# Threshold attention and a low-rank mixer on one core: every transpose of weights and u moved from the transfer engines to TensorE, and score steps paired across borders

## The chip, the core and the metric

The kernel runs on one core of one Trainium2 chip. The core has five engines that work through their own queues in order: TensorE (PE in the profile, with its weight loads as PEld), VectorE (DVE), ScalarE (ACT), GpSimd (POOL) and SyncE (SP), which issues transfers. Sixteen DMA engines move the data. The metric is the device time of one execution in microseconds (us).

## What is computed

Eight batches, eight heads, 576 rows, 64 columns per head. Attention keeps only the scores within tau of the row's largest, and its output goes through a mixer with a low-rank step over the rows and a two-layer network over the columns:

```python
def _attn_ref(q, k, v, tau):
    scores = scale * np.matmul(q, k.transpose(0, 1, 3, 2))
    thresh = np.max(scores, axis=-1, keepdims=True) - tau
    scores = np.where(scores >= thresh, scores, -1000000000.0)
    scores = scores - np.max(scores, axis=-1, keepdims=True)
    attn = np.exp(scores)
    attn = attn / (np.sum(attn, axis=-1, keepdims=True) + 1e-09)
    return np.matmul(attn, v)

def _moe_ref(x, U, V, w_ch1, w_ch2):
    h = x.transpose(0, 2, 1) @ U @ V              # rank 32, over the 576 rows
    u = x + h.transpose(0, 2, 1)
    return u + np.maximum(u @ w_ch1, 0.0) @ w_ch2  # 512 -> 2048 -> 512
```

q, k and v are float32; the result has shape 8 x 576 x 512 in float32.

## The kernel before

Heads are taken two at a time: four pairs of heads in each of 8 batches, 32 pairs `p`. A pair's 576 rows are four tiles of 128 and one of 64; two neighbouring pairs put their last 64 rows together, so a couple of pairs has nine score steps, and the kernel has 16 x 9 = 144. A step makes two tiles (one for each head, `x`) of 128x576.

The life of a step, with the lines of the profile:

- `scores` (L641): float32 matmuls of q and k into PSUM. A group has one step or two. PSUM has eight banks; a group of two steps takes the six of `trio`, a single group four. In the first couple all steps are single; in the other 15 couples the first is single and eight make four groups of two: 9 + 15 x 5 = 84 groups.
- `weigh` (L670, DVE): scales the scores out of PSUM, takes their extreme `m` along the row.
- `threshold` (L686, ACT): `m` plus tau. `exponential` (L693, ACT).
- `select` (L700, DVE): exponential where the score passes the threshold, else zero, into `w_ring` as bf16, with the row's sum into `den`.
- `twin` (L718, POOL): copies the last 64 columns once more, so that a tile has five blocks of 128.
- The turn, since the weighted sum needs keys on the partitions: `turn_w` (L724) is a transposing transfer on SP's queue; `turn_pe` (L731) is five matmuls against the identity into one bank, with a copy out of PSUM on ACT (`copy_w`, L741). In the kernel before, 25 of the 288 tiles go by PE: tile `x == 1` of steps 1 to 3 in the first `EARLY = 8` pairs, and one more. The other 263 go by 143 transfers, most of which take both tiles of a step.

`value_tasks` follows for each pair: the weighted sum `product` (L798 to 808) with v split in a high and a low bf16 part (`high` on ACT L600, `low` on POOL L607); the reciprocal of the sums (`inverse`, L774 and 776, DVE); for pairs 0 to 3 (`SOFT`) the product with it (L831), for the others a joining add (L859) and a product on POOL (L866); the low-rank step (L879, L894, L901); then u in bf16 (L908), which is turned for the mixer: in the first 8 pairs by PE and ACT (`turn_u` L916, `copy_u` L932), in the others by a transposing transfer (`send_u`, L922).

`mixer_tasks` of a batch has 16 tasks of four matmuls up (L998), the rests (L1014), with a relu on ACT (L988); then for each of nine row tiles of two batches four tasks of four matmuls down (L1031), a final sum on DVE (`finish`, L1043) and the store (L1054 to 1060, SP). These matmuls lie between the attention's on PE.

All of this is written down as tasks with an engine and what they depend on. Their order is not found at run time: `ORDER` is a list of task numbers, worked out beforehand, and `BANK` gives each PE task its PSUM bank. A negative number in `ORDER` is a filler matmul (L473) that computes nothing needed. Each engine's queue is in that order. q and k are loaded from POOL's queue for most pairs (L510), from SP's for pairs 1 and 2 (`LOADERS`); the mixer's weights come over POOL's queue, each held back by a `gate` on a score step.

Of the kernel before, what the change touches and what calls it, by code (L numbers as in the profile page):

```python
# [68 lines left out]
P = 128  # L69
FP32 = mybir.dt.float32  # L70
# [15 lines left out]
EARLY = 8  # L86
PHASES = (1, 2, 3, 4, 5, 6, 8, 28)
LONE = 2
LOADERS = (None, "SSSS", "SSSS")
ACTED = 0  # L90


W1_AT = (1, 4, 6, 9, 11, 14, 16, 19)
W2_AT = (20, 21, 23, 24, 25, 26, 28, 29)
# [14 lines left out]
PE, VEC, SCA, POOL, SP = range(5)  # L109
# [3 lines left out]
class Task:  # L113
# [17 lines left out]
    23, 21, 22, 25, 20, 26, 24, 19, 44, 28, 46, 40, 27, 29, 42, -1, -1, -1, -1, -1, -1, -1, -1, -1, 32, 41, 30, 33,  # L131
    43, 34, 31, 39, 35, 45, -2, -2, -2, 59, 201, 36, 200, 60, 37, 38, 204, 61, 63, -7, -7, -7, -7, -7, 69, 205, 62,
    65, 64, 206, 54, 70, 50, 198, 55, 52, 71, 203, 73, 218, 82, 66, 72, 202, 77, 222, 74, 199, 1, 83, 47, 67, 3, 84,
    49, 86, -3, -3, -3, -3, -3, -3, 95, 0, 78, 68, 85, 51, 87, 53, 90, 96, 75, 97, 219, 76, -8, -8, -8, -8, -8, -8,
    108, 91, 221, 98, 99, 2, 48, 211, 103, 109, 207, 209, 110, 112, 119, 100, 225, 212, 111, 104, 79, 114, 213, 120,
    92, 224, -3, 80, 121, 123, 220, -7, 129, 115, 125, 223, 113, 122, 4, 93, 131, 432, 56, 130, 101, 210, 88, 439,
    142, 89, 124, 137, 105, 81, 126, 57, 106, 102, 94, 143, 169, 132, 127, 144, 437, 146, 128, 155, 168, 214, 150,
    138, 107, 233, 170, 139, 231, 116, 157, 145, 438, 133, 117, 229, 156, 232, 457, 238, 134, 163, 455, 208, 151,
    158, 234, 171, 434, 230, 240, 159, 135, 58, 136, 239, 140, 244, 147, 152, 241, -6, 248, 141, 118, 172, 456, 242,
    245, 5, 243, 433, 153, 249, 453, 154, 250, 160, -8, -8, -8, -8, 173, 251, 164, 215, 161, 174, 256, 452, 261, -1,  # L140
    -1, -1, 184, 162, 148, 252, 262, 435, 264, 183, 149, 165, -4, 273, 257, 459, 175, 185, 246, 258, 253, 247, 216,
    274, 176, 254, 458, 275, 228, 177, 263, 268, 217, 286, -8, -8, 178, 255, 166, 259, 281, 179, 443, 454, 277, 269,
    188, 226, 436, 276, 287, 444, 227, 6, 180, 189, 265, 167, -3, -3, -3, -3, -3, -3, 181, 278, 288, 266, 289, 296,
    282, 270, 260, 267, 182, 290, 283, 291, 297, 441, 279, 271, 186, 292, 280, 300, 298, 272, 293, 345, 235, 440,
    344, 187, 299, 306, 294, 236, 302, 447, 445, 237, 307, 284, 448, 309, 346, 308, 301, 626, 446, 462, -2, -2, -2,
    318, 285, 303, 295, 190, 310, 304, 460, 313, 319, 191, 320, 9, 192, 322, -8, -8, 193, 331, 311, 347, 326, 624,
    312, 194, 321, 620, 334, 314, 349, 305, 195, 467, 348, 315, 625, 350, 468, 332, -4, 316, 351, 465, 333, 339,
    352, 335, 463, 353, 466, 196, 323, 336, 354, 317, 472, 355, 324, 464, 619, 325, 327, 356, 337, 622, 197, 474,
    357, 328, 338, 442, 623, 473, 364, 358, 461, 621, 329, 340, 475, 476, 482, 639, 359, 478, 341, 477, 640, 330,
    365, 8, 483, 342, 484, 360, 10, 343, 495, 7, 486, 362, 496, 449, 642, 479, 485, 507, 469, 363, 487, 490, 470,  # L150
    361, 498, 509, 480, 634, 366, 488, 481, 630, 471, 508, 632, 635, 631, 521, 367, 644, 633, 489, 520, 368, 497,
    511, -7, -7, 369, 491, 530, 522, 510, 370, 515, 492, 645, 499, 371, 887, 502, 531, 882, 372, 374, 532, 373, 12,
    493, 375, 494, 641, 380, 503, 533, 523, 376, 540, 504, 381, 11, 505, 525, 516, 378, 500, 377, 512, 886, 501,
    382, 506, 526, 450, 379, 384, 383, 541, 534, 13, 386, 524, 536, 513, 552, 535, 527, 514, 385, 537, 542, 883,
    387, 543, 528, 517, 538, 553, 646, 518, 547, 650, 554, 451, 519, 388, 529, 566, 555, 14, 390, 628, 565, 389,
    888, 651, 659, 544, 391, 556, 545, 884, 392, 546, 660, 560, 661, 394, 567, 568, 629, 548, 393, 669, 647, 561,
    395, 549, 539, 572, 557, 643, 665, 670, 562, 550, 558, 663, 648, 16, 396, 671, 551, 627, 885, 573, 398, 397,
    569, 672, 400, 662, 399, 682, 570, 673, 574, 402, 571, 881, 683, 401, 563, 674, 403, 652, 559, 654, 564, 578,
    577, 901, 598, 653, 666, 15, 655, 649, 575, 677, 694, 664, 579, 678, 685, 667, 580, 689, 679, 695, 581, 892,
    576, 696, 902, 684, 894, 698, 18, 707, 896, 582, 893, 690, 675, 897, 702, 586, 708, 676, 583, 599, 895, 584,  # L160
    587, 636, 585, 588, 717, 668, 686, 903, 600, 601, 589, 710, 691, 637, 712, 718, 17, 607, 590, 719, 603, 687,
    638, 697, 727, 608, 709, 680, 703, 656, 591, 904, 889, 692, 404, 699, 604, 907, 592, 890, 681, 609, 704, 406,
    602, 605, 688, 693, 728, 606, 405, 593, 765, 713, 906, 407, 723, 711, 908, 739, 766, 610, 594, 700, 611, 657,
    767, 701, 714, 595, 905, 740, 612, 658, 715, 912, 752, 613, 720, 596, 729, 614, 721, 741, 1048, 705, 911, 408,
    734, 1054, 722, 716, 597, 1049, 409, 724, 706, 1051, 753, 410, 742, 747, 725, 615, 1055, 726, 411, 730, 735,
    913, 914, 412, 743, 736, 769, 1053, 731, 915, 413, 616, 773, 744, 732, 770, 916, 737, 774, 748, 917, 617, 1072,
    755, 733, 921, 775, 754, 749, 764, 738, 771, 794, 776, 909, 618, 923, 768, 750, 795, 414, 922, 745, 759, 772,
    746, 796, 1068, 924, 415, 760, 751, 1071, 925, 891, 756, 931, 1050, 927, 926, 1052, 777, 785, 757, 932, 1075,
    786, 758, 933, 1070, 941, 778, 761, 934, 787, 416, 779, 942, 935, 780, 788, 898, 417, 781, 944, 928, 762, 950,
    763, 936, 929, 937, 418, 797, 782, 930, 899, 951, 946, 790, 789, 952, 900, 910, 960, 1063, 1059, 791, 954, 1061,  # L170
    792, 1057, 961, 783, 793, 943, 420, 1062, 1056, 938, 1069, 953, 784, 421, 1280, 947, 1064, 1060, 939, 970, 956,
    945, 1278, 940, 798, 955, 948, 957, 918, 949, 799, 962, 971, 919, 422, 800, 965, 1277, 972, 806, 1058, 974, 801,
    1073, 966, 423, 963, 1074, 807, 426, 958, 802, 920, 808, 959, 427, 981, 803, 1279, 973, 424, 428, 985, 1273,
    980, 804, 809, 964, 429, 805, 976, 975, 967, 811, 982, 810, 430, 1009, 968, 983, 986, 977, 989, 1010, 1078, 812,
    1011, 978, 1008, 1274, 979, 990, 1083, 1079, 991, 993, 969, 1013, 984, 1080, 425, 995, 813, 999, 987, 1014,
    1000, 843, 992, 988, 1084, 814, 1015, 1001, 1017, 996, 1002, 1088, 994, 1065, 1018, 1004, 1066, 1081, 1019,
    1003, 1016, 815, 1082, 1089, 844, 1037, 1020, 1090, 819, 997, 1038, 998, 1039, 1091, 1005, 816, 817, 1094, 1006,
    1098, 1076, 1012, 1092, 1095, 1293, 1007, 818, 1093, 1295, 820, 1021, 1099, 1275, 821, 431, 1276, 1100, 1022,
    822, 1298, 1029, 1028, 1077, 1108, 1023, 1104, 1067, 1024, 1109, 823, 1030, 1101, 1031, 1102, 1096, 1281, 1296,
    1105, 1117, 824, 1097, 1294, 1103, 1110, 1113, 1299, 1025, 1111, 1106, 1282, 1297, 1118, 1288, 1284, 1107, 1300,  # L180
    1119, 1289, 1286, 1285, 1127, 1033, 1441, 1287, 1128, 1123, 1040, 845, 1112, 1034, 1120, 1085, 1137, 1035, 1124,
    846, 1121, 1114, 1026, 1139, 1115, 825, 1129, 1447, 1130, 1116, 1138, 1036, 827, 1143, 1122, 1032, 826, 829,
    1148, 1140, 1141, 1125, 831, 1442, 1147, 1126, 830, 1086, 1131, 828, 847, 832, 1149, 1156, 1132, 1142, 1041,
    1133, 848, 1157, 1134, 1150, 1308, 1087, 1135, 1042, 1158, 1309, 1304, 1043, 1152, 1166, 1306, 1176, 1305, 1027,
    1167, 1467, 1307, 1175, 1440, 1168, 1044, 1151, 1159, 833, 1283, 1177, 1443, 1178, 1302, 1313, 1446, 1144, 834,
    1303, 1160, 1045, 1145, 1180, 1466, 1146, 1315, 1465, 1314, 835, 1181, 1445, 1169, 1153, 1323, 1461, 1162, 1161,
    1179, 1316, 1182, 836, 1163, 1171, 1184, 1324, 1319, 1164, 1444, 1204, 1325, 1185, 1317, 837, 1154, 1464, 1170,
# [186 lines left out]
def kernel(  # L374
# [24 lines left out]
    nc.vector.tensor_copy(out=identb, in_=ident)  # L399
    tau_t = consts.tile([P, 1], FP32, name="tau_t")  # L400
    nc.vector.memset(tau_t, tau_f)

    warm = consts.tile([P, 1], FP32, name="warm")
    nc.scalar.activation(out=warm, in_=tau_t, func=ACT.Exp)

# [761 lines left out]
```

## Time and profile before

| | before |
|---|---|
| median of 2 runs | 605.85 us (602.58 and 609.11) |
| the profiled execution | 601.79 us, span 600.0 us |
| HBM read, written | 37.90 MB, 9.44 MB |
| q1 (SP's and ACT's transfers) | 212,544 packets, 67.48 MB, 69.2% of 16 engines' span |
| q0 (POOL's transfers) | 13,408 packets, 21.58 MB, 17.7% |

The engines' busy times and the slices stand in the prediction. Some of the costliest groups, as the page has them:

```profile
L693 ACT ACTIVATE e_sb<-s_sb,m 128x576 bf16<-128x576 f32 x288 | 216.4, 776 | 37.6 <-DVE w_ring L700 25.9
L700 DVE SCALAR_TENSOR_TENSOR w_ring<-s_sb,thr,e_sb 128x576 bf16<-128x576 f32 x288 | 236.9, 849 | 6.4 <-DMA wT_ring<-w_ring 2.7
L670 DVE TENSOR_SCALAR_CACHE_REDUCE s_sb<-trio 128x576 f32<-128x576 f32 x288 | 205.9, 751 | 13.4 <-PE trio L641 11.3
L718 POOL COPY w_ring<-w_ring 128x128 bf16<-128x128 bf16 (+1 forms) x168 | 67.8, 410 | 127.5 <-DVE w_ring L700 85.9
L686 ACT ACTIVATE thr<-m,tau_t 128x2 f32<-128x2 f32 x144 | 41.5, 296 | 7.4 <-DVE s_sb L670 7.3
```

A row is: line, engine, operation, what is written from what, shape, number; then the busy time in us, the mean of one in ns; then the idle time of the engine just before such instructions and what ended most of it. A matmul's end is modelled, so neighbouring matmuls overlap in their busy times.

### The profile page before, as it was taken

To read this page: it belongs to the slowest core of one execution; us is meant where nothing else is said; L and a number is where in the kernel's file an instruction comes from. 1 tells how busy PE (TensorE), PEld (TensorE's weight loads), DVE (VectorE), ACT (ScalarE), POOL (GpSimd) and SP (SyncE) were. 2 spreads that over 40 slices of the span, in tenths; PEclk is the share of its full clock that TensorE was granted. 3 is DMA by queue.
4 is the path that set the end of the run, shared out by engine and by line. 5 is a ranking of instruction groups with operands and counts; after the bars stand their busy time and mean duration, and the time that the engine had idled before them with its cause. 6 is when DMAs were issued, how large, how long until landed. Compare 5 with 4: busy or idle time off the path is not lost. (4 is left out here: it accounts for less than half of the span.)

```text
span 600.0 us, 16926 instructions
## 1 busy us (share of the span) xinstructions
PE 574.2 (96%) x6150; PEld 346.3 (58%) x6221; DVE 515.7 (86%) x1399; ACT 459.4 (77%) x959; POOL 337.1 (56%) x580
## 2 busy tenths in 40 slices
PE   7999999899999998999999999999999999999996
PEld 4466655665665664656565665556655666555542
DVE  3999999999999999999999999999988999962002
ACT  3788999898898876997679986799786887683330
POOL 2987777787467558664567474576473544141000
PEclk9999999999999999999999999999999999999999
DMA  5999999986999899998898998998999877684203
GB/s 118 177 159 153 177 156 183 167 173 136 155 164 168 156 173 177 175 160 155 162 176 159 170 154 184 192 167 167 157 174 142 176 135 138 97 155 74 62 19 88
DMA packets 226996, 90.49 MB, mean 151 GB/s; under 512 B 205408, under 2 KB 217520, under 8 KB 226912
## 3 DMA queue, kind: packets, MB, share of 16 engines
q1 hardware_dynamic: 212544, 67.48, 69.2%
q0 software_dynamic: 13408, 21.58, 17.7%
q8 instruction: 49, 0.80, 0.6%
q10 hardware_dynamic: 960, 0.34, 0.2%
q14 instruction: 35, 0.29, 0.2%
HBM read 37.90 MB, written 9.44 MB: 79 GB/s over the span
## 5 line engine op out<-in xcount | busy, mean ns | idle before, releaser
L693 ACT ACTIVATE e_sb<-s_sb,m 128x576 bf16<-128x576 f32 x288 | 216.4, 776 | 37.6 <-DVE w_ring L700 25.9
L700 DVE SCALAR_TENSOR_TENSOR w_ring<-s_sb,thr,e_sb 128x576 bf16<-128x576 f32 x288 | 236.9, 849 | 6.4 <-DMA wT_ring<-w_ring 2.7
L670 DVE TENSOR_SCALAR_CACHE_REDUCE s_sb<-trio 128x576 f32<-128x576 f32 x288 | 205.9, 751 | 13.4 <-PE trio L641 11.3
L641 PE MATMUL trio<-qkT 64*64 64x288 f32 (+2 forms) x2304 | 162.3, 410 | 2.0 <-DVE s_sb L670 1.7
L718 POOL COPY w_ring<-w_ring 128x128 bf16<-128x128 bf16 (+1 forms) x168 | 67.8, 410 | 127.5 <-DVE w_ring L700 85.9
L641 PEld LDWEIGHTS trio<-qkT 64*64 64x64 f32 x2304 | 82.4, 132 | 57.9 <-issue 7.3
L1031 PEld LDWEIGHTS <-R 128*128 128x128 bf16 x576 | 53.5, 98 | 65.8 <-issue 12.1
L1031 PE MATMUL bank<-W2b,R 128*128 128x512 bf16 x338 | 84.6, 379 | 3.8 <-DVE o L1043 1.9
L510 POOL DMA_DIRECT2D qkraw<-in_q_dram x117 | 76.9, 659 | 10.0 <-PE bank L572 3.0
L510 POOL DMA_DIRECT2D qkraw<-in_k_dram x117 | 76.4, 655 | 10.7 <-PE bank L572 6.3
L998 PEld LDWEIGHTS <-W1b 128*128 128x128 bf16 x512 | 47.0, 98 | 53.6 <-issue 3.8
L866 POOL TENSOR_TENSOR x<-x,rec 128x256 f32<-128x256 f32 (+1 forms) x84 | 55.0, 660 | 38.4 <-DVE x L859 24.8
L607 POOL TENSOR_TENSOR vh<-vraw_ring,vh 64x128 bf16<-64x128 f32 (+1 forms) x64 | 54.0, 843 | 23.1 <-ACT vh L600 11.3
L998 PE MATMUL trio<-uT,W1b 128*128 128x512 bf16 x256 | 62.3, 379 | 1.4 <-ACT tt L885 0.4
L804 PEld LDWEIGHTS <-wT_ring 128*128 128x128 bf16 x896 | 55.7, 98 | 10.0 <-issue 6.1
L998 PE MATMUL bank<-uT,W1b 128*128 128x512 bf16 x223 | 58.2, 379 | 0.9
L988 ACT ACTIVATE R<-trio 128x512 bf16<-128x512 f32 x74 | 41.9, 599 | 15.5 <-PE trio L998 13.5
L1031 PE MATMUL trio<-W2b,R 128*128 128x512 bf16 x200 | 47.6, 379 | 2.4 <-ACT R L988 1.9
L686 ACT ACTIVATE thr<-m,tau_t 128x2 f32<-128x2 f32 x144 | 41.5, 296 | 7.4 <-DVE s_sb L670 7.3
L988 ACT ACTIVATE R<-bank 128x512 bf16<-128x512 f32 x70 | 40.7, 595 | 5.2 <-PE bank L1014 3.3
L804 PE MATMUL bank<-vh,wT_ring 128*128 128x128 bf16 x512 | 36.6, 219 | 0.0
L1043 DVE TENSOR_TENSOR o<-trio,x 128x512 f32<-128x512 f32 x13 | 8.9, 690 | 31.3 <-PE trio L1031 31.3
(105 smaller groups left out, 731.4 us busy)
## 6 DMA issues: line engine op xcount, KB each, us to landing
out_dram<-o SPq DMA_DIRECT2D x71, 128.0 KB, 2.8
vraw_ring<-in_v_dram SPq DMA_DIRECT2D x32, 160.0 KB, 3.5
qkraw<-in_k_dram POOLq DMA_DIRECT2D x59, 80.0 KB, 3.9
qkraw<-in_q_dram POOLq DMA_DIRECT2D x58, 80.0 KB, 4.0
vraw_ring<-in_v_dram SPq DMA_DIRECT2D x32, 128.0 KB, 4.1
qkraw<-in_q_dram POOLq DMA_DIRECT2D x59, 64.0 KB, 4.0
qkraw<-in_k_dram POOLq DMA_DIRECT2D x58, 64.0 KB, 3.9
W1b<-in_moe_w_ch_dram POOLq DMA_DIRECT2D x8, 256.0 KB, 5.0
```

Of the source, the lines that this page charges most:

```text
L510: queue.dma_start(pr.qkraw[part, to, j, :], src[:, j, of, :])
L607: nc.gpsimd.tensor_tensor(out=pr.vh[part, tiles_, :, h, :], in0=raw[part, tiles_], in1=pr.vh[part, tiles_, :, 0, :], op=ALU.subtract)
L641: mm = nc.tensor.matmul(cols[part, lo:hi], a.tT[hs, 0, rows], a.tT[hs, 1, lo:hi], start=True, stop=True)
L670: nc.vector.tensor_scalar(out=s_sb, in0=score_cols(slot, x), scalar1=-scale, scalar2=None, op0=ALU.mult, op1=ALU.min, accum_out=m[:, x:x + 1])
L693: nc.scalar.activation(out=e_sb, in_=s_sb, func=ACT.Exp, bias=m[:, x:x + 1], scale=-1.0)
L700: nc.vector.scalar_tensor_tensor(out=w_sb[:, 0:S], in0=s_sb, scalar=thr_[:, x:x + 1], in1=e_sb, op0=ALU.is_le, op1=ALU.mult, accum_out=pr. ...
L718: nc.gpsimd.tensor_copy(out=w_sb[:, xs, S:640], in_=w_sb[:, xs, 512:S])
L804: nc.tensor.matmul(av[:, 2 * a + j, :], w, pr.vh[:, kt, j, :, :], start=kt == 0, stop=False)
L866: nc.gpsimd.tensor_tensor(out=x, in0=x, in1=over_sum(part), op=ALU.mult)
L988: nc.scalar.activation(out=R2[:, fts, lo:hi], in_=bank[t.got[0]].rearrange("p (f c) -> p f c", c=hi - lo), func=ACT.Relu)
L998: nc.tensor.matmul(bank[t.got[0]], W1b[:, dt, ft * P:(ft + 1) * P], bt.uT[:, dt, :], start=(dt == 0), stop=(dt == 3))
L1031: nc.tensor.matmul(ch, R2[:, ft, lo:lo + P], W2b[:, ft, :], start=(ft == 0), stop=(ft == 15))
```

## The change

1. `turn_w` and `send_u` are gone: all 288 weight tiles and all 32 u are turned by PE. The tile `x == 0` is copied out of PSUM by ACT, `x == 1` by DVE (`COPIED`). The twin is copied for each tile by itself.
2. What a border between two couples leaves over is scored together with the next couple's first step: 9 single groups, 67 of two and one single, 77 groups.
3. Work moves between engines: thresholds from ACT to POOL (`THRESH = 32`, all pairs), the high part of v from ACT to POOL (`HIGH = 32`, all), the add of 1e-9 from DVE to ACT, the products of pairs 0 to 3 from DVE to ACT and POOL (`ACTED = 4`), the final sums of batches 0 to 6 from DVE to ACT and POOL (`SHARED = 7`: 31 of 36).
4. q and k of pairs 1 to 6 are loaded over SP's queue. The weights' loads follow one another in POOL's order instead of a gate, and mixer matmuls wait only for the pieces that they read.
5. `ORDER` and `BANK` are new: 3,879 tasks and 43 fillers for 3,284 and 56.

```diff
-EARLY = 8
+COPIED = (SCA, VEC)
-LOADERS = (None, "SSSS", "SSSS")
-ACTED = 0
+LOADERS = (None,) + ("SSSS",) * 6
+SHARED = 7
+THRESH = 32
+HIGH = 32
+ACTED = 4
...
+        def top(_):
+            nc.gpsimd.tensor_copy(out=pr.vh[:, :, :, 0, :], in_=raw)
+
-        t = done["vhi", p] = add(SCA, 0.62, high,
+        t = done["vhi", p] = add(*(POOL, 1.1, top) if p < HIGH else (SCA, 0.62, high),
...
+        def level(_):
+            nc.gpsimd.tensor_scalar(out=thr_, in0=m, scalar1=tau_f, scalar2=None, op0=ALU.add)
+
-        thr = add(SCA, 0.19, threshold, mins)
+        thr = add(POOL, 0.2, level, mins, lock=0.03) if p < THRESH else add(SCA, 0.19, threshold, mins)
...
-            both = not (p < EARLY and 1 <= i < 4)
...
-            twin_ = add(POOL, 0.235 if both else 0.18, twin, [sel] + ([first_sel] if both else []), lock=0.03)
-
-            def turn_w(_, xs=slice(0 if both else x, x + 1)):
-                to = pr.wT[:, xs, :, i * P:(i + 1) * P] if i < 4 else wT4[:, xs, :, HB:HB + P]
-                nc.sync.dma_start_transpose(
-                    to.rearrange("p x k r -> p (x k) r"),
-                    w_ring[n % (NW // 2)][:, xs, :].rearrange("p x c -> p (x c)"))
+            def twin(_, x=x):
+                w_sb = w_ring[n % (NW // 2)]
+                nc.gpsimd.tensor_copy(out=w_sb[:, x, S:640], in_=w_sb[:, x, 512:S])
+
+            ready = add(POOL, 0.18, twin, [sel], lock=0.03)
...
+            t = done["wT", tiles[0]] = add(PE, 0.28, turn_pe, [ready] + free, banks=1, kind="wT")
+
+            def copy_w(_, x=x, t=t, on=nc.vector.tensor_copy if COPIED[x] == VEC else nc.scalar.copy):
+                on(out=pr.wT[:, x, :, i * P:(i + 1) * P] if i < 4 else wT4[:, x, :, HB:HB + P],
+                   in_=bank[t.got[0]][:, 0:320].bitcast(BF16).rearrange("p (k r) -> p k r", k=NT))
+
+            t = add(COPIED[x], 0.42 if COPIED[x] == VEC else 0.575, copy_w, [t], frees=[t])
...
+        def guard(_):
+            nc.scalar.activation(out=pr.rec, in_=pr.den, func=ACT.Identity, bias=eps_t[:, 0:1], scale=1.0)
+
         def inverse(_):
-            nc.vector.tensor_scalar(out=pr.rec, in0=pr.den, scalar1=1e-9, scalar2=None,
-                                    op0=ALU.add)
             nc.vector.reciprocal(out=pr.rec, in_=pr.rec)
...
-        if p < EARLY:
-            uT_ = done["uT_", p] = add(PE, 0.23, turn_u, deps, banks=1, kind="uT")
-        else:
-            done["uT_", p] = done["uT", p] = add(SP, 1.3, send_u, deps, dma=0.9)
+        uT_ = done["uT_", p] = add(PE, 0.23, turn_u, deps, banks=1, kind="uT")
...
-            t = add(PE, 0.862, up, uT + weights1 + done.get(("o", b - 2), []), banks=1, kind="p1",
+            t = add(PE, 0.862, up, uT + weights1[ft // 8 * 4:ft // 8 * 4 + 4] + done.get(("o", b - 2), []), banks=1, kind="p1",
...
+            def hold(_, halves=halves, o=o):
+                nc.scalar.copy(out=o, in_=bank[halves[0].got[0]])
+
+            def plus(_, i=i, o=o):
+                nc.gpsimd.tensor_tensor(out=o, in0=o, in1=bt.x[:, i, :] if i < 4 else bt.x4, op=ALU.add)
+
+            if b < SHARED:
+                t = add(SCA, 0.485, hold, [halves[-1], outs[0], got("sum")], frees=[halves[0]])
+                t = done["sum"] = add(POOL, 1.1, plus, [t, got("sum")], lock=0.03)
+            else:
+                t = done["sum"] = add(VEC, 0.603, finish, [halves[-1], outs[0], got("sum")],
+                                      frees=[halves[0]])
...
+    held = []
     for p in range(0, NP, 2):
+        nine = [(p, i) for i in range(NT)] + [(p + 1, i) for i in range(4)]
         prepare_tasks(p)
+        if held:
+            score_tasks(*held, nine.pop(0))
+            held = []
+            close(p - 1)
         prepare_tasks(p + 1)
...
+        while nine:
+            n = 1 if p < LONE else 2
+            if len(nine) < n and p + 2 < NP:
+                held = nine
+                break
+            score_tasks(*nine[:n])
+            nine = nine[n:]
+        close(p)
+        if not held:
+            close(p + 1)
```

## The prediction

> **What bounds the kernel now.** I read the page's busy table first, with the slices for the granted clock and the transfers.
>
> ```profile
> span 600.0 us, 16926 instructions
> ...
> PE 574.2 (96%) x6150; PEld 346.3 (58%) x6221; DVE 515.7 (86%) x1399; ACT 459.4 (77%) x959; POOL 337.1 (56%) x580
> ...
> PEclk9999999999999999999999999999999999999999
> DMA  5999999986999899998898998998999877684203
> ```
>
> PE is busy for 96% at a full clock, and the transfer engines are nearly full too, until the last eighth. The table of stretches, cut where the last score group ends, separates two stages.
>
> ```profile
> 0.00:525.00 525.00, 505.95 (x5717) 310.63 (x5781) 495.92 (x1356) 430.24 (x902) 329.28 (x568) 1.00 0.95 161
> 525.00:600.00 75.00, 68.27 (x434) 35.65 (x440) 19.82 (x44) 29.19 (x58) 7.87 (x12) 1.00 0.41 80
> ```
>
> Columns: PE, PEld, DVE, ACT, POOL, clock, transfer share, GB/s. While scores run, PE (506 of 525) and DVE (496) are both near full; behind that lie 75 us of mixer matmuls, which the chain of waits shows as PE alone. Busy matmuls have modelled ends, so I looked in the timeline at when the next one starts.
>
> ```profile
> 48.03 0.45 PE L731 MATMUL trio<-identb,w_ring 128*128 128x128 bf16 x5 [0.45 <-DVE s_sb L670]
> 48.32 0.44 PE L731 MATMUL bank<-identb,w_ring 128*128 128x128 bf16 x5
> 48.60 0.61 PE L572 MATMUL trio<-ident,qkraw 128*128 128x128 f32 x4
> ```
>
> A turn of one weight tile is "busy" for 0.45 us but holds PE for 0.29 (48.03 to 48.32) and 0.28. Counted so, the program's own matmuls before come to: 1,096 of 512 columns at 0.216 (four in 0.86 in the chain) 237; 320 weighted sums at 0.25 (505.34 to 505.60) 80; 60 double score groups at 2.11 (timeline, 508.45 to 510.56) and 24 single at 1.13 (66.71 to 67.84) 154; q/k turns 32; rests 14; low rank and spreading 16; turns and u 10; fillers 12. That is 555 of 600 us. So PE really is the bound, with 45 us of waits, drains, start and end.
>
> By the Trainium skill ("Perfetto Trace Analysis", Identifying the Most-Contended Engine), matmul busy share is a poor measure and the weight-load share should be read instead. That is 58% here and would leave room for everything added, a time of about 602; the spacing in this timeline speaks against it.
>
> **The change, part by part.** The profiled execution took 601.8 us (span 600.0 plus 1.8), 4 below the median of two, 605.85; the sum starts from 601.8.
>
> *Turns on PE.* The 144 steps have 288 weight tiles; 25 were turned by PE, now all. 263 more at 0.29 = +76 (0.28 to the busy row's 0.45: +74 to +118; I take the back-to-back starts, since PE's queue has other work behind each). u: 24 more at 0.23 (82.11 to 82.34) = +5.5. Fillers fall from 56 to 43: 13 at about 0.25 = -3.3. Seven pairs of single groups become doubles: 7 x (2 x 1.13 - 2.11) = -1.1. PE: **+77**. Nothing else leaves PE.
>
> The skill prices a 128x128 transpose in a kernel at about 275 ns ("TensorE: Matmul & The Clock Gate", Part 4: PE-mode transpose), a rule that speaks against this change: 1,411 more would be an estimated 388 us. The rows above have five in 0.28.
>
> *Transfers.* 143 weight and 24 u transposes leave SP, with SP's 100 us of waiting on the twin copies. SP takes 32 more q/k loads from POOL (q/k of pairs 3 to 6), queued early with value loads and few stores. Who waited on the transposes? DVE's select for 2.7 us in total, PE's weighted sums of the first pairs (L808) for 3.3. So the gain is 0 to 6 us; I take 0.
>
> *DVE.* 144 copies out of PSUM, 128x640 bf16. No such row. Bounds:
>
> ```profile
> L1043 DVE TENSOR_TENSOR o<-bank,x 128x512 f32<-128x512 f32 x23 | 15.7, 684 | 6.3 <-PE bank L1031 6.2
> L859 DVE TENSOR_TENSOR x<-bank,x 128x256 f32<-128x256 f32 x32 | 13.5, 421 | 2.1 <-ACT x L855 1.9
> L859 DVE TENSOR_TENSOR x<-bank,x 64x128 f32<-64x128 f32 x15 | 4.1, 285 | 0.6 <-ACT x L855 0.3
> L399 DVE CAST identb<-ident 128x128 bf16<-128x128 f32 x1 | 0.2, 163 | 0.0
> ```
>
> 256 elements more cost 0.263 us, so 640 at one a cycle take 0.82; at two a cycle (320) 0.49. The one single-source copy (L399) is 0.12 under the two-source row of its length, so I take 0.49, +71 (0.82: +118). Off DVE: 32 adds of L774 at 0.214 (6.9), 31 of 36 final sums at 0.687 (21.3), 12 products of L831 (4.3). Net +38 (up to +85). In the first stage, where 26 of the sums lie, that is 496 + 42 = 538; at its present 94.5% that stage takes 569, and 77 behind it make 646: under PE, so hidden. The copy's price decides only from about 0.67.
>
> On PSUM sources the skill ("VectorE: DVE Perf Modes", the perf-mode tier table) caps copies at two a cycle, an estimated 0.46 us; no row here shows it.
>
> *ACT.* Off: 144 thresholds at 0.296 (41.5), 32 casts of v (23.1). On: 119 copies of weight tiles at 0.69 (82), 24 of u at 0.58 (14), 31 of sums at 0.59 (18), 32 guards at 0.28 (9), 12 at 0.34 (4). 459 + 63 = 522, 78% of the new time: hidden unless it is late.
>
> *POOL.* On: 288 half twins for 168 at 0.39 (+44), 144 thresholds (0.10 of the smallest memset to 0.30 of the 32x64 cast; 0.25: 36), 32 casts of v (0.85 to 1.45; 1.2 by the 128x512 row of L607: 38), 31 sums at 1.2 (37), 12 products (8); off, 32 load issues at 0.66 (21). 337 + 142 = 479. In the first stage 329 becomes about 465, from 63% to 78% of it. Hidden on average, but POOL works in order: a threshold now stands behind 1.2 us instructions, and DVE's select behind the threshold. The twin feeds PE's turn the same way, and behind a late turn stand the mixer's matmuls. Cost 0 to 27 here; taken 0 in the sum.
>
> *PSUM and borders.* Each turn holds a bank until its copy; while a double group holds six, two remain. Late copies would stop PE: 0 to 20 us, taken 0. The four steps left over at a border join the next couple's first step, so the odd pair's sums start about one group later (525 / 84 = 6 us): 0, covered by the mixer's matmuls, up to that 6 at a border without them. Weight loads are issued by order instead of a gate, and the mixer waits for only its own: L998 showed no wait for them, so 0.
>
> *What PE can win back.* PE was idle for 19 us in the first stage, 7.7 of them in the first 75 us, where DVE starts the pipeline; turns can run there. I take 6. Sum: 601.8 + 77 - 6 = **673**.
>
> **Rivals.**
> - *DVE becomes the bound.* Copies at 0.82: 538 + 47 = 585 in the first stage, at 94.5% 619, plus 77: 696. For: DVE is as full as PE there. Against: L399's row.
> - *POOL's queue becomes the wait.* For: POOL's rise to 78%, in order, on the path of every select; DVE waited for thresholds on ACT only 1.6 us in all. If each of 144 is late by one 1.2 us instruction and half of it reaches DVE: 538 + 86 = 624, plus 77: 701. It decides from a delay of about 0.8 us each.
> - *Not slower: the turns ride in PE's pauses.* Place: PE's 26 us of idle and the modelled ends inside its busy time. Price: about 603 if everything fits. It decides only if 61 of the 77 us vanish (618, 2% above before), but 555 + 77 = 632 of matmuls, back to back, already exceed that; so a turn would have to hold PE for under 0.23 with no wait left anywhere. The trace shows 0.28 and 0.29. That PE is not turning all tiles is excluded: the program has 1,440 such matmuls.
>
> **Chances and numbers.** PE carries it, 650 to 688: 0.66. DVE 0.11, POOL 0.15, both about 690 to 715. Not slower 0.04 (0.02 faster). Slower still but with less than 77 added, under 650: 0.04. The low end, 650, is 679 less all 26 of idle and 3 of cheaper turns; the high end, 706, takes in both rivals' prices. About 2% can be told from no change here. Predicted 673, range 650 to 706; faster 0.02, same 0.02, slower 0.96.
>
> **What would show it.** PE stays at 95% or more busy, with the turn group at 1,440 matmuls and starts 0.28 to 0.30 apart; the transfer digits fall by more than half; the last score group ends near 597 with 75 us behind it. DVE's copy row at 0.49 or under confirms that term; at 0.67 or more, with PE idle before DVE, DVE's rival holds. Selects that wait for POOL's threshold by tens of us show the POOL rival. A turn that starts the next matmul after less than 0.2 us would make the prediction wrong.

## The result and the profile after

The changed kernel takes 691.23 us (two runs, 690.74 and 691.71) where the kernel before takes 605.85: a ratio of 1.1409 [1.1143, 1.1676], or 85 us slower. The forecast was 673 in a range of 650 to 706. The profiled execution took 691.7 us, of which the span is 689.9. The kernel before was timed again beside the experiments, with medians of 603.56 to 605.18; against 605.1 the change costs 86.

The page of the changed kernel, from its first, second and fourth parts (the last line is the chain of waits, the work that ended last followed back to what released it):

```profile
span 689.9 us, 19776 instructions
...
PE 652.5 (95%) x7537; PEld 425.6 (62%) x7619; DVE 554.8 (80%) x1469; ACT 521.9 (76%) x1001; POOL 453.8 (66%) x887
...
PEclk9999999999999999999999999999999999999999
DMA  8664252422103132131122213323021321110223
...
PE 57%; DVE 16%; ACT 7%; POOL 7%; issue 7%; DMA 4%; SPq 2%; another core or an unknown queue 0%; POOLq 0%; DVEq 0%; ACTq 0%
```

PE's work has grown from 574.2 to 652.5 us, by 78, and the transfer engines have emptied. But the span grew by 90, so 12 us more of it are idle on PE (25.8 before, 37.4 after), and the chain of waits runs through PE for only 57%.

The table of stretches of the changed kernel, cut at the end of its last score group (columns as in the prediction: PE, PEld, DVE, ACT, POOL, clock, transfer share, GB/s):

```profile
0.00:615.00 615.00, 583.23 (x7055) 387.59 (x7129) 540.99 (x1439) 488.31 (x935) 439.28 (x865) 1.00 0.29 67
615.00:690.00 75.00, 69.27 (x485) 38.04 (x491) 13.78 (x31) 33.56 (x66) 14.50 (x22) 1.00 0.20 45
```

The 75 us behind the scores are as they were. All of the growth lies in the first stage: PE waits there for 31.8 of 615 us, where it waited for 19.1 of 525.

The turns in the timeline of PE in the changed kernel (start, busy time, then the instruction; x5 is one weight tile):

```profile
244.25 0.45 PE L773 MATMUL trio<-identb,w_ring 128*128 128x128 bf16 x5
244.54 1.03 PE L1057 MATMUL bank<-W2b,R 128*128 128x512 bf16 x4
245.41 1.00 PE L773 MATMUL trio<-identb,w_ring 128*128 128x128 bf16 x15
246.25 1.89 PE L1057 MATMUL bank<-W2b,R 128*128 128x512 bf16 x8
```

One tile holds PE for 0.29 us (244.25 to 244.54) and three hold it for 0.84. The price of a turn is the forecast one.

The groups of the changed kernel with shapes kept apart (busy time, mean ns of one | idle time before, what ended it):

```profile
L755 DVE SCALAR_TENSOR_TENSOR w_ring<-s_sb,thr,e_sb 128x576 bf16<-128x576 f32 x288 | 242.0, 863 | 17.9 <-POOL thr L742 5.0 <-ACT e_sb L748 4.3 <-PE trio L773 3.0
...
L773 PE MATMUL trio<-identb,w_ring 128*128 128x128 bf16 x855 | 71.2, 219 | 6.3 <-DVE s_sb L725 3.1 <-POOL w_ring L766 2.3 <-DVE wT L781 0.4
...
L773 PE MATMUL bank<-identb,w_ring 128*128 128x128 bf16 x585 | 51.1, 219 | 4.1 <-DVE x L936 1.3 <-DVE wT_ring L781 1.1 <-ACT o L1073 0.8
L781 ACT COPY wT_ring<-trio 128x640 bf16<-128x640 bf16 x71 | 48.8, 693 | 7.3 <-PE trio L773 5.8 <-DVE wT_ring L781 1.4
L742 POOL TENSOR_SCALAR thr<-m 128x2 f32<-128x2 f32 x144 | 44.5, 309 | 43.0 <-DVE s_sb L725 33.6
L1076 POOL TENSOR_TENSOR o<-o,x 128x512 f32<-128x512 f32 x31 | 40.9, 1323 | 19.7 <-ACT o L1073 19.2
...
L781 DVE COPY wT_ring<-trio 128x640 bf16<-128x640 bf16 x78 | 37.3, 484 | 18.3 <-PE trio L773 13.2 <-ACT wT_ring L781 4.3
L667 POOL CAST vh<-vraw_ring 128x640 bf16<-128x640 f32 x32 | 26.5, 828 | 3.2 <-PE trio L696 1.0 <-PE trio L835 0.8 <-DMA vraw_ring<-in_v_dram 0.6
```

The turns stand behind 10.4 us of PE's idle time (6.3 and 4.1), put down to work of DVE (among it the copies that empty the banks), of ACT and of POOL's twin (L766). The 25 turns of the kernel before stood behind 1.0 us:

```profile
L731 PE MATMUL bank<-identb,w_ring 128*128 128x128 bf16 x80 | 7.3, 220 | 0.5 <-POOL w_ring L718 0.3
L731 PE MATMUL trio<-identb,w_ring 128*128 128x128 bf16 x45 | 4.0, 220 | 0.5 <-DVE s_sb L670 0.5
```

So some 9 of the 12 us by which PE's idle time grew lie directly before turns. DVE's copy out of PSUM takes 0.484 us, the lower of the two prices that the prediction weighed. The select waits for POOL's threshold for 5.0 us in all.

### The profile page after: what moved, and what is told of

Its sections match the earlier page's. It is cut to its first block, busy times and chain, and to the rows that moved or that the text cites. A ratio compares the mean times of both kernels' runs of the same rounds, so it can differ in the third digit from the quotient of the medians.

```text
span 689.9 us, 19776 instructions
## 1 busy us (share of the span) xinstructions
PE 652.5 (95%) x7537; PEld 425.6 (62%) x7619; DVE 554.8 (80%) x1469; ACT 521.9 (76%) x1001; POOL 453.8 (66%) x887
## 3 DMA queue, kind: packets, MB, share of 16 engines
q1 hardware_dynamic: 36320, 23.58, 14.5%
## 4 chain that ended last, share of the span: by engine, by line
PE 57%; DVE 16%; ACT 7%; POOL 7%; issue 7%; DMA 4%; SPq 2%; another core or an unknown queue 0%; POOLq 0%; DVEq 0%; ACTq 0%
PE trio L696 12%; DVE w_ring L755 8%; PE trio L1057 8%; PE trio L1024 7%; DVE s_sb L725 6%; PE bank L1057 5%; PE bank L1024 5%; PE trio L773 4%; PE bank L839 3%; PE trio L839 3%; PE bank L773 3%; ACT e_sb L748 3%; POOL qkraw L563 2%; DVE wT_ring L781 2%; POOL x L901 1%
## 5 line engine op out<-in xcount | busy, mean ns | idle before, releaser
L755 DVE SCALAR_TENSOR_TENSOR w_ring<-s_sb,thr,e_sb 128x576 bf16<-128x576 f32 x288 | 242.0, 863 | 17.9 <-POOL thr L742 5.0
L766 POOL COPY w_ring<-w_ring 128x64 bf16<-128x64 bf16 x288 | 89.6, 328 | 84.4 <-DVE w_ring L755 74.9
L773 PEld LDWEIGHTS <-w_ring 128*128 128x128 bf16 x1440 | 91.6, 98 | 48.7 <-issue 15.8
L773 PE MATMUL trio<-identb,w_ring 128*128 128x128 bf16 x855 | 71.2, 219 | 6.3 <-DVE s_sb L725 3.1
L563 POOL DMA_DIRECT2D qkraw<-in_q_dram x101 | 67.4, 668 | 9.5 <-PE bank L625 5.5
L742 POOL TENSOR_SCALAR thr<-m 128x2 f32<-128x2 f32 x144 | 44.5, 309 | 43.0 <-DVE s_sb L725 33.6
L1057 PE MATMUL bank<-W2b,R 128*128 128x512 bf16 x268 | 68.3, 379 | 1.8 <-issue 0.5
L563 POOL DMA_DIRECT2D qkraw<-in_k_dram x101 | 67.4, 668 | 3.8 <-issue 2.1
L1057 PE MATMUL trio<-W2b,R 128*128 128x512 bf16 x271 | 68.3, 379 | 1.4 <-ACT R L1014 0.7
L773 PE MATMUL bank<-identb,w_ring 128*128 128x128 bf16 x585 | 51.1, 219 | 4.1 <-DVE x L936 1.3
```

What stands on the lines that cost most here:

```text
L563: queue.dma_start(pr.qkraw[part, to, j, :], src[:, j, of, :])
L755: nc.vector.scalar_tensor_tensor(out=w_sb[:, 0:S], in0=s_sb, scalar=thr_[:, x:x + 1], in1=e_sb, op0=ALU.is_le, op1=ALU.mult, accum_out=pr. ...
L766: nc.gpsimd.tensor_copy(out=w_sb[:, x, S:640], in_=w_sb[:, x, 512:S])
L773: nc.tensor.transpose(ps[:, kt * P:(kt + 1) * P], w_sb[:, kt * P:(kt + 1) * P], identb)
L1057: nc.tensor.matmul(ch, R2[:, ft, lo:lo + P], W2b[:, ft, :], start=(ft == 0), stop=(ft == 15))
```

## The experiments

The theory at the start: PE's longer work sets the time, and all else is hidden. The rivals: DVE's copies, POOL's queue, and, once 691 was known, hand-overs between the engines. In brackets behind a time stands the median of the kernel before, timed beside it. Differences are taken from the changed kernel's 691.23, which was not timed beside these runs; the medians of the kernel before differ by up to 2 us, so a difference of that size says nothing.

**One block instead of five (e1).** Each turn writes one 128x128 block in place of five, and the copy spreads that block over all five; four of the five blocks of every turned tile are left out.

```diff
-                for kt in range(NT):
+                for kt in range(1):
...
-                   in_=bank[t.got[0]][:, 0:320].bitcast(BF16).rearrange("p (k r) -> p k r", k=NT))
+                   in_=bank[t.got[0]][:, 0:64].bitcast(BF16).unsqueeze(1).to_broadcast([P, NT, P]))
```

> PE turns one of the five blocks of a weight tile, and the copies read that block five times: 1,152 of the 1,440 turn matmuls are left out, the copies, twins, banks and the order stay. If PE's time is what the change cost (theory 1), 1,152 x 0.056 = 64 us go: 691 becomes about 627 to 632, PE still 93% or more busy. If POOL's queue or DVE's copies hold PE back (theories 2 and 3), their work is the same and PE only waits more: 680 or above.

Measured: 686.53 (before 604.37), 1.1342 [1.1257, 1.1428]. 1,152 matmuls at 0.056 us, some 64 us of PE, are gone and give back under 5, not the 59 to 64 that PE's time alone would have given. The page of e1, busy times and chain:

```profile
PE 615.4 (90%) x6393; PEld 371.4 (54%) x6467; DVE 557.9 (81%) x1469; ACT 520.9 (76%) x1001; POOL 456.6 (66%) x887
...
PE 34%; DVE 30%; ACT 12%; issue 9%; POOL 9%; DMA 3%; SPq 2%; DVEq 0%; POOLq 0%; ACTq 0%
```

And its first stage in the table of stretches:

```profile
0.00:612.00 612.00, 546.77 (x5942) 335.08 (x6009) 543.22 (x1437) 487.48 (x935) 442.14 (x865) 0.98 0.30 67
```

PE now waits for 65 of 612 us, twice as long as with all five blocks. The granted clock in this stage is 0.98 where it was 1.00, so PE's remaining work also ran slower: an estimated 10 us (2% of 547) of the 64; a turn's matmul takes up to 314 ns there, and up to 230 in the changed kernel. No engine's row is full, and the chain passes from PE (34%) to DVE (30%), ACT and POOL and back: a second limit stands at about 685 us (at a full clock up to 10 less, by this estimate). That it is a round through several engines and not one of them is read from the chain.

**Every turn twice (f1).** The other side of the same question; each tile is turned twice into the same bank.

```diff
-                for kt in range(NT):
+                for kt in [*range(NT)] * 2:
```

> Each tile is turned twice into the same bank, 1,440 matmuls more, 81 us of PE; copies and order as in the changed kernel. Relief of PE by 64 us gave back only 3 to 5 us, so PE alone is not the bound. Theory A (PE is full at this point and only another limit lies just under it): 691 + 70 to 81 = 760 to 772. Theory B (DVE and the hand-overs set the time, PE fits under them): less than 40 us more, 731 or below.

Measured: 750.09 (605.18), 1.2375 [1.2261, 1.2488], between the two expectations. The 1,440 additional matmuls (81 us at 0.056) cost 59; PE's idle time falls from 37 to 19 us. The chain of waits of f1:

```profile
PE 85%; DVE 4%; DMA 3%; POOL 3%; SPq 2%; ACT 2%; issue 2%; DVEq 0%; POOLq 0%; ACTq 0%
```

With more on PE, PE is most of the chain (85%); with less, only a third of it. By these two runs the changed kernel sits at the bend between the two.

**Back to transfers (e2, e3, f3).** One of a step's two tiles, or both, is turned by a transposing transfer again. In e2 (x = 0) and e3 (both) the transfer stands at the copy's place in the order, where the next step may already have written the same ring tile, so that part of the turned weights are another step's. In f3 it stands at the turn's place, and nothing at the copy's. The edit of e2:

```diff
+            sent = x == 0        # e3: True
-            t = done["wT", tiles[0]] = add(PE, 0.28, turn_pe, [ready] + free, banks=1, kind="wT")
+            t = done["wT", tiles[0]] = add(PE, 0.28, (lambda _: None) if sent else turn_pe, [ready] + free,
+                                           banks=1, kind="wT")
...
-            t = add(COPIED[x], 0.42 if COPIED[x] == VEC else 0.575, copy_w, [t], frees=[t])
+            t = add(COPIED[x], 0.42 if COPIED[x] == VEC else 0.575, turn_w if sent else copy_w, [t], frees=[t])
```

> The 144 tiles of x = 0, which ACT copied, go back to transposing transfers on SP, one for each tile; the other 144 stay with PE and DVE. Theory 1 (PE's time): 144 x 0.28 = 40 us go, with the waits of these turns (10 us for 288) 45: 645 to 652. Theory 2 (POOL's thresholds and twins): these are unchanged, 685 or above. Theory 3 (the copies): ACT loses 100 us of copies, DVE none: 685 or above.

> All 288 weight tiles go by transfer, one for each tile; u stays with PE, and the moved work and the 77 groups stay. Theory 1: 288 x 0.28 = 81 us of PE go, with the turns' waits 90: 600 to 612, within 2% of before, so the other parts of the change are worth next to nothing. If the moves to POOL or the pairing cost by themselves (theory 2): 620 or more. If DVE's share was a bound (DVE is 39 us under before here): 590 or less.

> As the run with all tiles by transfer, but each transfer stands where the changed kernel's order has the turn on PE, before the next step may write the same ring tile; in the earlier run it stood at the copy's place, later. PE loses 81 us, DVE 70, ACT 100. If the turns with their copies are the whole cost: 600 to 612. If the order, worked out for turns of 0.28 us and not for transfers of several us, is what counts (theory C): 640 or more, with DVE's select or the weighted sums waiting for the transfers.

Measured: e2 752.93 (604.37), 1.2439 [1.2344, 1.2535]; e3 848.12, 1.4002 [1.3925, 1.408]; f3 808.71 (605.18), 1.3342 [1.3201, 1.3482]. One line of the table of waits (total, count, longest) of e3, then of f3:

```profile
DVE w_ring L755 <- DMA wT_ring<-w_ring: 150.9, 50, 9.2
```

```profile
DVE w_ring L755 <- DMA wT_ring<-w_ring: 108.4, 41, 9.2
```

The transfers took about 3 us to land (up to 6.9), the turns 0.28. In the kernel before they took 4.7 (up to 9.7), mostly two tiles at a time, and yet its selects waited for them for 2.7 us in all: its order gives them that time. The order of the changed kernel does not, so the ring is not free when the next select comes. The granted clock was lower too, 0.95, 0.90 and 0.92 in e2, e3 and f3, so part of the added time is PE's own work at a slower clock. These three runs therefore do not price the transfers that the change removed; they show only that one part can't be undone inside an order made for another.

**Thresholds back on ACT (e4).** `THRESH = 32` becomes `THRESH = 0`.

> The 144 thresholds go back from POOL to ACT, in the same order; POOL loses 44 us, ACT gains 42. Theory 1: PE's work is the same, 691 within 8 either way. Theory 2 (a threshold behind long POOL instructions holds DVE's select, and the twin behind it PE's turn): POOL's waits on this path go, 680 or less.

Measured: 692.38 (604.37), 1.1438 [1.1388, 1.1488], 1 us from the changed kernel. Its busy times:

```profile
PE 654.7 (95%) x7537; PEld 427.4 (62%) x7619; DVE 552.0 (80%) x1469; ACT 546.8 (79%) x1145; POOL 402.7 (58%) x743
```

POOL's work falls from 453.8 to 402.7 us and ACT's rises from 521.9 to 546.8. Moving the thresholds off POOL gains nothing here that can be measured, in keeping with the 5.0 us of wait above.

**A smaller copy on DVE (f2).** DVE copies one of five blocks of its tiles; the rest stays zero.

```diff
+                kn = 1 if x else NT
-                on(out=pr.wT[:, x, :, i * P:(i + 1) * P] if i < 4 else wT4[:, x, :, HB:HB + P],
+                on(out=pr.wT[:, x, 0:kn, i * P:(i + 1) * P] if i < 4 else wT4[:, x, 0:kn, HB:HB + P],
```

> DVE copies only the first of the five blocks of each of its 144 tiles, the other four blocks of these weights stay zero (cleared once at the start, about 5 us of DVE before the first score): DVE loses about 40 us, the turns on PE stay. Theory A: 691 within 6. Theory B (DVE's amount of work sets the time): 650 to 660. Theory C (the round through banks and rings in the fixed order, several engines long): 675 to 688.

Measured: 688.62 (605.18), 1.136 [1.1256, 1.1465]. Its busy times:

```profile
PE 657.9 (96%) x7619; PEld 426.7 (62%) x7619; DVE 527.8 (77%) x1471; ACT 521.2 (76%) x1001; POOL 447.3 (65%) x887
```

27 us off DVE give back 2.6, hardly more than the kernel before varies: DVE is not the bound by itself.

**Turns and copies both cut (g3).** One block turned, one block copied, on DVE and on ACT; the rest stays zero.

> The changed kernel with both sides of the turn cut: one of five blocks is turned and copied, on DVE and on ACT; the other four blocks of the weights stay zero (cleared at the start, about 5 us). PE loses 64 us, DVE 28, ACT about 60; twins, thresholds, banks and order stay. The turns' matmuls alone gave back 4, DVE's copies alone 3. If PE and the copies were two limits side by side, both on the way: 640 to 655. If the rest of the round (scores, select, POOL's thresholds and twins, banks in fixed order) is as long by itself: 675 to 688.

Measured: 658.09 (605.1; two runs), 1.0879 [1.0775, 1.0982], between the two expectations. Its busy times:

```profile
PE 601.5 (92%) x6393; PEld 363.2 (55%) x6467; DVE 526.6 (80%) x1471; ACT 462.7 (70%) x1001; POOL 456.1 (69%) x887
```

Cutting turns gave 5, cutting DVE's copies 3; cutting turns and all copies gives 33. So limits stand side by side, and cutting one leaves another. Which the other one is, is not separated: g3 also takes 59 us off ACT, and no run cuts ACT's copies alone.

**No twin (f4).** POOL's half twin of each weight tile is not made; those columns stay zero.

```diff
-            ready = add(POOL, 0.18, twin, [sel], lock=0.03)
+            ready = add(POOL, 0.18, lambda _: None, [sel], lock=0.03)
```

> The 288 copies of the twin are left out, the 64 columns they fill stay zero (so the upper half of the fifth key block is zero): POOL loses 90 us and the turn follows the select directly, one hand-over less. Theory A and B: 691 within 6. Theory C with POOL on the round: 670 or below.

Measured: 702.78 (605.18), 1.1594 [1.1487, 1.1701]: 61 us off POOL, and 11.6 (1.7%) slower, which neither expectation had. The busy times of f4, and DVE's select among its groups with shapes apart:

```profile
PE 661.6 (94%) x7619; PEld 427.3 (61%) x7619; DVE 571.8 (82%) x1469; ACT 522.1 (75%) x1001; POOL 392.7 (56%) x603
...
L757 DVE SCALAR_TENSOR_TENSOR w_ring<-s_sb,thr,e_sb 128x576 bf16<-128x576 f32 x288 | 260.7, 927 | 13.1 <-ACT e_sb L750 4.0 <-PE trio L775 3.4 <-POOL vh L662 1.4
```

The same select takes 927 ns in the mean where it took 863, which is 18.7 us for 288 of them. The twin is thus no cost that can be had back by leaving it out; why the selects grow longer is not shown by this run, and the last section comes back to it.

**The change's parts, put into the kernel before (g1, g2, h1).** Instead of undoing, each part is added to the kernel before, whose order and transfers stay. g1 adds 1,312 matmuls of 128 columns that nobody needs (73 us on PE), in the tasks of the mixer (up), the weighted sums and the low-rank step, ahead of the matmuls that overwrite them; unlike turns they add no hand-over of their own:

```diff
+                for _ in range(5):
+                    nc.tensor.matmul(bank[t.got[0]][:, 0:P], identb, identb, start=True, stop=True)
```

> The kernel before with PE work alone added: 1,312 matmuls of 128 columns against the identity, five before each task of matmuls up and each weighted sum, three before each low-rank and spreading task, into the bank that the task then overwrites; 1,312 x 0.056 = 73 us, as many as the turns of the changed kernel add. No copy, bank, hand-over or order changes. Theory A (PE's amount, as predicted): 605 + 70 to 80 = 675 to 685. Theory C (PE has slack between hand-overs): 650 or less.

g2 moves work as the change does, with no turn added: thresholds and the high part of v to POOL, the guard to ACT, the final sums of seven of the eight batches to ACT and POOL; the products of pairs 0 to 3 stay where they were. Two of these edits:

```diff
-            nc.scalar.activation(out=thr_, in_=m, func=ACT.Identity,
-                                 bias=tau_t[:, 0:1], scale=1.0)
+            nc.gpsimd.tensor_scalar(out=thr_, in0=m, scalar1=tau_f, scalar2=None, op0=ALU.add)
...
+                if b < 7:
+                    nc.scalar.copy(out=o, in_=bank[halves[0].got[0]])
+                    nc.gpsimd.tensor_tensor(out=o, in0=o, in1=bt.x[:, i, :] if i < 4 else bt.x4, op=ALU.add)
+                    return
```

> The kernel before with the moved work alone: thresholds and the high part of v from ACT to POOL, the add of 1e-9 from DVE to ACT, the final sums of batches 0 to 6 to ACT and POOL; the transposes stay on the transfer engines, the order is that of before. POOL gains about 115 us, DVE loses 28, ACT 37. Theory A: 600 to 612. Theory C with POOL on the round (thresholds behind 1.2 us instructions hold the select): 620 or more.

h1 does both.

> The kernel before with both: the 1,312 added matmuls of 128 columns on PE (alone 605 to 664) and the moved work on POOL and ACT (alone 605 to 642); transposes on the transfer engines, order of before. If the two costs add up, since a hand-over that comes late leaves PE without its next task and PE has no room to catch up: 605 + 59 + 37 = 695 to 702. If they lie side by side, the longer covering the other: 664 to 674. The changed kernel took 691.

Measured: g1 664.47 (605.1; two runs), 1.0984 [1.0875, 1.1093], +59, between its two expectations. g2 641.91 (605.1), 1.0627 [1.0533, 1.0721], +37. h1 681.10 (603.56), 1.1285 [1.1243, 1.1327], +78, again between. The page of g1, busy times and chain:

```profile
PE 643.7 (97%) x7450; PEld 420.2 (63%) x7533; DVE 518.6 (78%) x1399; ACT 465.2 (70%) x959; POOL 335.4 (50%) x580
...
PE 83%; DVE 4%; DMA 3%; issue 3%; ACT 2%; POOL 2%; SPq 1%; DVEq 0%; POOLq 0%; ACTq 0%
```

The page of g2, busy times and DVE's select, and one line of its table of waits:

```profile
PE 586.7 (92%) x6150; PEld 350.4 (55%) x6221; DVE 510.2 (80%) x1337; ACT 437.6 (68%) x846; POOL 458.1 (71%) x787
...
L702 DVE SCALAR_TENSOR_TENSOR w_ring<-s_sb,thr,e_sb 128x576 bf16<-128x576 f32 x288 | 253.7, 904 | 24.8 <-POOL thr L689 17.9
...
DVE rec L777 <- ACT rec L776: 15.1, 24, 3.0
```

In g1 only PE has more to do, and PE is 83% of the chain: 73 us of work cost 59, the rest fits into waits that were there. In g2 no engine but POOL has more to do, and POOL is busy for only 71%, yet 37 us come. DVE's select waits for the threshold on POOL for 17.9 us and takes 904 ns instead of 849, some 16 us more; and the reciprocal on DVE waits for the guard on ACT for 15.1 us, a wait that the kernel before, with both steps on DVE, did not have. At a granted clock of 0.988 PE's unchanged work also shows 586.7 us for 574.2. Which of the moves in g2 costs how much was not separated. The busy times of h1:

```profile
PE 647.9 (95%) x7450; PEld 421.1 (62%) x7533; DVE 512.6 (75%) x1337; ACT 441.5 (65%) x846; POOL 451.5 (66%) x787
```

h1 lies between the larger part alone (59) and the sum of the two (96): of the moved work, 18 us are not covered by PE's longer work.

## Why the prediction was right, and where its sum was short

The direction and the main term were right, and the time lies in the range. But 691 is just above the 650 to 688 that the prediction gave to its own account, "PE carries it", and inside the 690 to 715 that it gave to the two rivals. That the range held it is owed to the rivals' prices, which set its upper end, and neither rival happened as it was priced; so much of it is luck.

- *PE's term.* Forecast +77, measured +78.3 busy; a tile's turn 0.28 to 0.29; 75 us behind the last score group. All as forecast. But the work is not the cost: g1 shows 73 us of matmuls of the same size costing 59. The prediction let PE win back 6 us; in g1 it won back 14.
- *Against the page.* The Trainium skill's price of about 275 ns for one transpose ("TensorE: Matmul & The Clock Gate", Part 4: PE-mode transpose) would have made an estimated 388 us of the added turns. In this trace a turn's matmul has a duration of 219 ns, and the next one starts 56 ns later (five in 0.28 us, fifteen in 0.84) at a granted clock of 1.0; the spacing is what holds PE here, so the measurement decides. The weight-load share, which the prediction set against the spacing, rose from 58% to 62% while the span grew by 90 us: the room that it suggested was not there.
- *DVE's term.* Forecast 0.49 a copy and 554 busy, measured 0.484 and 554.8. The copy's price of 0.82, and with it DVE's rival as priced, falls; f2 gives back 2.6 us for 27.
- *ACT* 522 forecast, 521.9 measured. *POOL* 479 forecast, 453.8 measured: the twins take 89.6 us in all and not the 112 of the forecast, the casts of v 0.828 each and not 1.2, while thresholds (0.309 for 0.25) and final sums (1.323 for 1.2) are dearer.
- *The transfers.* Taken at no gain; their queue went from 69.2% to 14.5% of the span and the time got longer. A gain of a few us inside the sum is not excluded: no run here removes the transfers alone.
- *Hand-overs.* "Taken 0" for POOL's queue and for banks is the term that was short. The first stage ended near 615 and not near 597, and these 18 us are the whole miss: the sum had PE's idle time fall by 6, and it grew by 12, of which some 9 stand directly before turns (10.4 us against 1.0). By turn that is no more than before, 0.04 us: the 263 added turns at the wait of the 25 would have been an estimated 10.5 us, a term that the prediction left at 0. That hand-overs can cost as much is shown in the kernel before: there the moved work costs 37 us by itself and 18 beside PE's (g2, h1). But these 18 are not the changed kernel's: in its order moving the thresholds back gains nothing (e4), and the wait for the guard is 3.7 us and not 15.1. How its own 86 us divide among turns, moves, twins, banks and copies is open.
- *POOL's rival*, 701, came near the time with a mechanism that did not occur, so its nearness is chance. Its sum also left out the 5.5% of DVE's idle time that the sum of DVE's rival has; with it, it would be 569 + 86 + 77 = 732. In the changed kernel the selects hardly wait for thresholds (5.0 us, and e4 changes nothing); in the order of before they do (g2, 17.9 us). The order of the changed kernel was worked out with the thresholds on POOL; that this is why, is not shown.
- *"PE carries it, the rest is hidden"* is thus the larger part of the cause and not all of it. Added to the kernel before, PE's work alone (73 us of it) costs 59, where the change costs 86. Taken out of the changed kernel (e1, 64 us of it), it gives back 5; g3 fits the reading that by then the rest of the round is about as long as PE's work.

## What to carry to other kernels

In this kernel several engines run in a fixed order, three of them busy for 76% or more and POOL for 56 to 66%. Work added to the fullest one was paid for the most part (59 of 73 us in g1, 59 of 81 in f1), and "hidden" work on the others was not free (37 us in g2): price it by adding it alone to the kernel before. Undoing a part inside the new kernel can mislead twice, since another limit may stand just beneath (64 us of PE gave 5) and since an order made for one latency punishes another (0.28 to 3 us: 117 us more in f3, 157 in e3). Price a matmul by the distance between starts (0.29 us for a turn here), not by its busy time (0.45).

## What the hardware showed beyond that

DVE's select, which reads two operands in SBUF, has a median of 814 ns in the changed kernel, but single ones are held far longer: 1.9 us there, 2.7 before, 3.3 in g2, 3.9 in f4 and 5.1 in e1. The excess over 815 ns, summed over the 288 selects, is about 11 us before, 15 after, 27 in g2 and 34 in f4. The long ones go with a busy POOL: during selects of over 1.1 us (12 before, 18 after, 39 in g2, 35 in f4) POOL is busy for 93 to 99% of the time on average, during the others for 58 to 73%. The timeline of e1 shows the longest one on DVE:

```profile
357.93 5.06 DVE L755 SCALAR_TENSOR_TENSOR w_ring<-s_sb,thr,e_sb 128x576 bf16<-128x576 f32 x1
362.92 0.08 DVE L755 DVE_READ_ACCUMULATOR w_ring<-s_sb,thr,e_sb 128x1 f32 x1
```

and POOL at that time:

```profile
357.39 0.71 POOL L563 DMA_DIRECT2D qkraw<-in_q_dram  x1
358.13 1.28 POOL L1076 TENSOR_TENSOR o<-o,x 128x512 f32<-128x512 f32 x1
359.34 0.24 POOL L766 COPY w_ring<-w_ring 128x64 bf16<-128x64 bf16 x1
359.54 1.15 POOL L660 TENSOR_TENSOR vh<-vraw_ring,vh 128x512 bf16<-128x512 f32 x1
360.64 0.64 POOL L563 DMA_DIRECT2D qkraw<-in_q_dram  x1
361.26 0.67 POOL L563 DMA_DIRECT2D qkraw<-in_k_dram  x1
361.95 0.41 POOL L901 TENSOR_TENSOR x<-x,rec 64x128 f32<-64x128 f32 x1
362.32 1.80 POOL L1076 TENSOR_TENSOR o<-o,x 128x512 f32<-128x512 f32 x1
```

Through the whole of this select POOL has one instruction directly behind another, three of them issues of transfers. POOL's next instruction follows without a gap as well (362.32), and the select ends inside it, so the end of POOL's row of instructions is not what released it; what did is not shown. The Trainium skill ("SBUF — State Buffer", SBUF: two separate sides) describes a port pair that a DVE instruction with two SBUF inputs and a GpSimd instruction that reads SBUF share as an exclusive lock for the whole instruction; these rows agree in kind, but here the select spans several POOL instructions and not one. Whether this is also why f4 is slower, with POOL's long instructions at other moments once it no longer waits for its twins, no run here separates.
